# Local-global attention and a two-layer MLP on one core: q in 16-row partitions, a bank of its own for global-key scores, and a fixed order in two phases

## The chip, the cores and the metric

The kernel runs on one core of a Trainium2 chip. The metric is the device time of one execution in microseconds (us). TensorE runs the matmuls (PE in the profile, PEld its weight loads), VectorE is DVE, ScalarE is ACT, GpSimd is POOL, and SP issues the loads of v and the stores. TensorE's results go to PSUM, where the kernel's pools hold eight tiles of 128 x 512 fp32, called banks here.

## The reference

Eight batches of eight heads, 512 local and 32 global tokens of 64 features. Global queries look at all keys; local queries look at the 32 global keys and at local keys at most 32 positions away. The result goes through a two-layer MLP with weights 512 x 2048 and 2048 x 512.

```python
s_g  = scale * q_g @ [k_g, k_l].T;  out_g = softmax(s_g) @ [v_g, v_l]
s_ll = where(|i - j| <= 32, scale * q_l @ k_l.T, -1e9)
s_l  = concat([scale * q_l @ k_g.T, s_ll])
out_l = softmax(s_l) @ [v_g, v_l]
x = concat([out_g, out_l]) as [4352, 512]        # 8 * (32 + 512) rows
h = x @ w_in;  g = h / (1 + exp(-1.702 * h));  result = g @ w_out
```

## The kernel before

Four heads of a batch form a "quad", so there are 16 quads, two per batch. A quad does two rounds of score matmuls, three "value units" (`ov`: the sum of the exponentials, then the two halves of the features) and one output for the global queries (`og`). An "h step" makes 128 of the 2048 hidden features of 512 tokens (4 matmuls); an "o step" is a quarter of the sum for 128 output rows (4 matmuls). Batch i of x has 16 h steps and 16 o steps. The order of emission is reordered automatically per engine before it is built.

```python
psS = pool("psS", bufs=4, PSUM); psV = pool("psV", bufs=1, PSUM)      # scores; value units and og
psH = pool("psH", bufs=2, PSUM); psO = pool("psO", bufs=1, PSUM)      # h; o
qf = q_l.rearrange("b (u j) (n r t) d -> (b u) j r n (t d)", j=4, n=8, t=2)

def load(Q):
    for name, src in (("rk", kf), ("rq", qf)):
        r = ld.tile([128, 8, 2 * D], BF16, name=name)
        for j in range(4):
            nc.gpsimd.dma_start(out=r[32 * j : 32 * j + 32], in_=src[Q, j])

def load_v(Q):                       # ... loads vst from SP, then casts it:
    if Q < 4: nc.scalar.activation(v[:, :, : 4 * D], st, AF.Copy)
    else:     nc.gpsimd.tensor_copy(v[:, :, : 4 * D], st)

# start: load(0), globals, v0, load(1), masks, v1, w_in, load(2), v2, load(3), v3, w_out, ...

def quad(Q):                         # ... transposes of k and q, 2 rounds of scores
    for unit in range(3):
        ov = psV.tile([128, 512], F32, name="ov")
        for i, (e, q0, wd) in enumerate(pieces):       # global keys: 160, 160, 160, 32 columns
            nc.tensor.matmul(ov[:, q0 : q0 + wd], lhsT=lg, rhs=e, start=(i == 0), stop=False)
        for c in range(4):
            for j in range(4):                          # local keys, 32-column tiles
                nc.tensor.matmul(ov[32 * j : 32 * j + 32, q0 : q0 + wd], lhsT=lv, rhs=..., ...)
        # ... unit 0: reciprocal of the sums on VectorE; units 1, 2: product into x on VectorE

LAG = 24
for _ in batch(0): pass
for k in range(NBK * FC + LAG):
    i, st = divmod(k, FC)
    if i < NBK: h_step(i, st)
    if 0 <= k - LAG < NBK * FC: o_step(*divmod(k - LAG, FC))
    # ... and 12 pieces of the attention of batch i + 1, spread over the 16 steps;
    #     batch(b), from b = 1 on, expands the global keys of batch b + 1 with four products on GpSimd
```

The softmax here doesn't subtract the row's maximum and nothing guards it: scores larger than these inputs give would overflow.

## Time and profile before

| | before |
|---|---|
| time, median of the first 3 runs | 389.32 us (386.23 to 392.86) |
| TensorE busy | 347.3 us, 89% of the span |
| GpSimd busy | 135.8 us |
| period of one batch from 151 us on | 37.87 us |
| first h matmul / first o matmul starts | 36.95 / 77.8 us |

Lines of the page of before: busy time and instruction counts of each engine, then TensorE's busy tenths and its granted clock (in tenths) in 40 slices of about 9.7 us each, then the shares of the engines in the chain that ended last.

```profile
PE 347.3 (89%) x2960; PEld 178.4 (46%) x2960; DVE 223.8 (58%) x362; ACT 188.3 (48%) x375; POOL 135.8 (35%) x205
...
PE   0396777999999979999999999999999999999984
...
PEclk9999999899699998999999999999999999999999
...
PE 62%; DMA 11%; POOL 8%; ACT 8%; issue 6%; DVE 5%; ACTq 0%; DVEq 0%; POOLq 0%
```

Busy time of each engine of before in four stretches (from:to, length, then busy us and instruction count of each engine, the granted clock, the DMA share and GB/s).

```profile
core 0: us, PE busy (x) PEld busy (x) DVE busy (x) ACT busy (x) POOL busy (x), PEclk, DMA share, GB/s
0.00:30.00 30.00, 13.77 (x112) 8.15 (x116) 12.63 (x41) 13.19 (x21) 22.08 (x46) 1.00 1.25 181
30.00:75.00 45.00, 33.84 (x292) 17.32 (x285) 28.29 (x46) 17.06 (x35) 29.71 (x45) 0.96 1.16 132
75.00:151.00 76.00, 69.89 (x691) 36.11 (x689) 59.38 (x80) 40.73 (x84) 54.59 (x75) 0.93 0.80 104
151.00:209.00 58.00, 57.75 (x537) 29.65 (x538) 35.21 (x57) 32.32 (x67) 27.39 (x37) 1.00 0.54 93
```

From 151 us on TensorE has almost no idle time left (57.75 us busy of 58) and the clock is full. Before that it looks busy too, but this number misleads. The Trainium skill (Perfetto Trace Analysis, Identifying the Most-Contended Engine) says that matmul busy time is no good measure of distance from the limit, and here it isn't: between 75 and 151 us TensorE counts 69.89 us busy of 76, yet the matmuls that started in that stretch are worth only 58 us when each is counted at the pitch of the steady stage (0.864 us for four of 512 columns). The count of work is made from how many matmuls of each line have started by a moment:

| by, us | h, batches | o, batches | scores, quads | value units, quads |
|---|---|---|---|---|
| 30 | 0.00 | 0.00 | 2.00 | 0.17 |
| 50 | 0.19 | 0.00 | 2.00 | 2.00 |
| 75 | 1.00 | 0.00 | 3.59 | 2.33 |
| 151 | 2.59 | 1.06 | 8.00 | 7.00 |
| 209 | 4.12 | 2.62 | 10.84 | 10.00 |

A batch of h or of o is 13.8 us of streaming. The scores of a quad are about 1.84 us and its three value units about 2.2 us, read from the steady stage below (with the global output 0.56 us more, which I count with the units: 2.8).

The timeline of before in the steady stage, TensorE only (start, length, engine, line, operation, output<-inputs, shapes, count). A length runs to the modelled end of the last matmul, so the pitch is read from one start to the next.

```profile
216.23 0.23 PE L273 MATMUL ov<-e_2803,onesBD 128*128 128x160 bf16 x1
...
216.55 0.34 PE L280 MATMUL ov<-e_2803,ones_138 128*32 128x160 bf16 x8
...
216.97 1.04 PE L322 MATMUL hp<-xL,w_in_sb 128*128 128x512 bf16 x4
...
218.80 0.48 PE L231 MATMUL s<-qT,kT 32*128 32x192 bf16 x16
219.21 0.40 PE L253 MATMUL s<-qgBD_171,kT 128*128 128x128 bf16 x4
```

A value unit takes 216.97 - 216.23 = 0.74 us: 0.32 us for the four pieces with the global keys (`onesBD`), 0.42 us for the 16 tiled matmuls. Sixteen score matmuls take 219.21 - 218.80 = 0.41 us.

### The profile page before, as it was taken

The numbers are of one execution on the slowest core, as the hardware profiler recorded it, in microseconds if no ns is written. First come the engines' busy times: TensorE is split into PE (matmuls) and PEld (weight loads), VectorE is DVE, ScalarE is ACT, GpSimd is POOL, SyncE is SP. The second block draws the span as 40 slices with busy tenths as digits, with TensorE's granted clock in tenths as the row PEclk, the third lists the DMA queues.
The fourth block names the chain that finished last, engine by engine and source line by source line (L and its number), as shares of the span: only waits on it lengthen the run. The fifth ranks groups of instructions, "written<-read, shape, count | busy, mean of one in ns | idle before, by whom it ended". The sixth has DMA issues, their size and how long they took to land.

```text
span 389.2 us, 7403 instructions
## 1 busy us (share of the span) xinstructions
PE 347.3 (89%) x2960; PEld 178.4 (46%) x2960; DVE 223.8 (58%) x362; ACT 188.3 (48%) x375; POOL 135.8 (35%) x205
## 2 busy tenths in 40 slices
PE   0396777999999979999999999999999999999984
PEld 0253433544544434555555555555455544455531
DVE  4434359776797794658656855685545644333200
ACT  2462236625556843386448544854485443434311
POOL 8857937277890995826530011000000000000000
PEclk9999999899699998999999999999999999999999
DMA  9999999119992685936713000000101100111112
GB/s 155 190 189 179 112 185 145 12 34 175 172 106 59 104 116 57 135 83 83 112 51 83 29 28 29 29 29 28 49 7 38 45 29 27 40 43 54 53 57 54
DMA packets 83314, 31.15 MB, mean 80 GB/s; under 512 B 75856, under 2 KB 77904, under 8 KB 83280
## 3 DMA queue, kind: packets, MB, share of 16 engines
q0 software_dynamic: 44496, 13.38, 32.7%
q1 hardware_dynamic: 38784, 17.31, 18.3%
q8 instruction: 23, 0.38, 0.4%
q14 instruction: 11, 0.09, 0.1%
HBM read 35.13 MB, written 8.91 MB: 113 GB/s over the span
## 4 chain that ended last, share of the span: by engine, by line
PE 62%; DMA 11%; POOL 8%; ACT 8%; issue 6%; DVE 5%; ACTq 0%; DVEq 0%; POOLq 0%
PE op L337 26%; PE hp L322 21%; PE s L231 4%; DMA w_in_sb<-in_moe_w_in_dram 4%; PE ov L280 4%; PE s L253 4%; POOL rk L77 3%; POOL rq L77 3%; DMA rk<-in_k_l_dram 2%; DMA rq<-in_q_l_dram 2%; PE ov L273 2%; DMA w_out_sb<-in_moe_w_out_dram 2%; ACT ob L341 2%; ACT xg L305 2%; ACT th L325 2%
## 5 line engine op out<-in xcount | busy, mean ns | idle before, releaser
L322 PE MATMUL hp<-xL,w_in_sb 128*128 128x512 bf16 x512 | 136.9, 391 | 9.8 <-DVE gT L326 9.7
L337 PE MATMUL op<-w_out_sb,gT 128*128 128x512 bf16 x544 | 138.5, 381 | 3.7 <-ACT ob L341 2.8
L325 ACT ACTIVATE th<-hp 128x512 f32<-128x512 f32 (+1 forms) x144 | 83.0, 579 | 113.2 <-PE hp L322 111.2
L326 DVE SCALAR_TENSOR_TENSOR gT<-th,hp 128x512 bf16<-128x512 f32 (+1 forms) x144 | 93.4, 652 | 66.7 <-ACT th L325 66.1
L337 PEld LDWEIGHTS <-gT 128*128 128x128 bf16 x544 | 53.1, 98 | 67.5 <-issue 9.3
L322 PEld LDWEIGHTS <-w_in_sb 128*128 128x128 bf16 x576 | 53.3, 99 | 66.0 <-issue 16.9
L231 PE MATMUL s<-qT,kT 32*128 32x160 bf16 (+1 forms) x512 | 29.6, 252 | 16.8 <-DVE qT L216 14.2
L77 POOL DMA_DIRECT2D rk<-in_k_l_dram x64 | 37.2, 589 | 16.0 <-DVE kT L216 7.3
L77 POOL DMA_DIRECT2D rq<-in_q_l_dram x64 | 36.6, 577 | 8.2 <-DMA rq<-in_q_l_dram 3.0
L305 ACT ACTIVATE xg<-og,rg 32x64 bf16<-32x64 f32 x64 | 19.5, 305 | 30.2 <-DVE rg L301 29.6
L231 PEld LDWEIGHTS <-kT 32*128 32x128 bf16 x512 | 16.2, 96 | 33.5 <-issue 20.8
L341 ACT ACTIVATE ob<-op 128x512 f32<-128x512 f32 x34 | 20.5, 603 | 21.9 <-PE op L337 21.9
L293 DVE TENSOR_TENSOR xL<-ov,rs 128x512 bf16<-128x512 f32 x32 | 21.9, 686 | 8.3 <-PE ov L280 8.1
L216 DVE STREAM_TRANSPOSE kT<-rk 128x1024 bf16<-128x1024 bf16 x16 | 21.1, 1320 | 6.4 <-DMA rk<-in_k_l_dram 5.4
L216 DVE STREAM_TRANSPOSE qT<-rq 128x1024 bf16<-128x1024 bf16 x16 | 20.7, 1296 | 4.9 <-DMA rq<-in_q_l_dram 4.9
L287 DVE STREAM_TRANSPOSE sT<-ov 128x512 f32<-128x512 f32 x16 | 11.4, 711 | 7.6 <-PE ov L280 7.6
L306 DVE STREAM_TRANSPOSE xG<-xg 128x64 bf16<-128x64 bf16 x16 | 3.9, 246 | 19.8 <-ACT xg L305 19.8
L91 POOL CAST v_89<-vst 128x1024 bf16<-128x1024 f32 x3 | 3.1, 1040 | 28.3 <-issue 28.3
L291 DVE STREAM_TRANSPOSE rs<-rT 128x512 f32<-128x512 f32 x16 | 11.3, 708 | 0.5
L253 PEld LDWEIGHTS <-kT 128*128 128x128 bf16 x128 | 8.0, 100 | 7.6 <-issue 4.9
L186 POOL DMA_DIRECT2D w_in_sb<-in_moe_w_in_dram x16 | 8.5, 533 | 4.8 <-DMA w_in_sb<-in_moe_w_in_dram 4.3
L322 PE MATMUL hp<-xG,w_in_sb 128*128 128x256 bf16 x64 | 9.8, 273 | 0.1
(364 smaller groups left out, 347.9 us busy)
## 6 DMA issues: line engine op xcount, KB each, us to landing
vst<-in_v_l_dram SPq DMA_DIRECT2D x64, 128.0 KB, 4.6
out_dram<-ob SPq DMA_DIRECT2D x32, 256.0 KB, 2.0
rk<-in_k_l_dram POOLq DMA_DIRECT2D x64, 64.0 KB, 3.2
rq<-in_q_l_dram POOLq DMA_DIRECT2D x64, 64.0 KB, 3.7
w_in_sb<-in_moe_w_in_dram POOLq DMA_DIRECT2D x16, 128.0 KB, 7.1
w_out_sb<-in_moe_w_out_dram POOLq DMA_DIRECT2D x4, 512.0 KB, 9.2
out_dram<-ob SPq DMA_DIRECT2D x8, 64.0 KB, 1.7
rkg<-in_k_g_dram POOLq DMA_DIRECT2D x1, 192.0 KB, 12.6
```

The costliest lines, as they stand in the source:

```text
L77: nc.gpsimd.dma_start(out=r[32 * j : 32 * j + 32], in_=src[Q, j])
L216: nc.vector.transpose(dst.rearrange("p h (n r t) -> p h n t r", n=8, t=2), src.rearrange("p n (t h d) -> p h n t d", t=2, h=2),)
L231: nc.tensor.matmul(ps[j][:, col : col + wd], lhsT=kT[p, h, 128 * c : 128 * c + 128], rhs=qT[p, h, q0 : q0 + wd], start=(h == 0), stop=(h = ...
L253: nc.tensor.matmul(o, lhsT=l(h), rhs=r(h), start=(h == 0), stop=(h == 1), skip_group_check=True)
L280: nc.tensor.matmul(ov[32 * j : 32 * j + 32, q0 : q0 + wd], lhsT=lv, rhs=E[c // 2][:, j, col : col + wd], start=False, stop=(c == 3), skip_ ...
L293: nc.vector.tensor_mul(x[:, 2 * u + h, :], ov, rs)
L305: nc.scalar.activation(xg[p, :], og[p, j * D : (j + 1) * D], AF.Copy, scale=rg[p, j : j + 1])
L322: nc.tensor.matmul(hp[:, :n], lhsT=w_in_sb[:, kc, fc * 128 : (fc + 1) * 128], rhs=(xL[i] if i < B else xG)[:, kc, :], start=(kc == 0), sto ...
L325: nc.scalar.activation(th[:, :n], hp[:, :n], AF.Tanh, scale=0.851)
L326: nc.vector.scalar_tensor_tensor(gTs[i][:, fc, :n], in0=th[:, :n], scalar=1.0, in1=hp[:, :n], op0=ALU.add, op1=ALU.mult)
L337: nc.tensor.matmul(ops[i], lhsT=gTs[i][:, fc, tci * 128 : tci * 128 + 128], rhs=w_out_sb[:, fc, :], start=(fc == 0), stop=(fc == FC - 1))
L341: nc.scalar.activation(ob, ops[i], AF.Copy, scale=0.5)
```

## The change

Its intent: fewer and longer DMA runs for q, one 512-column matmul for global keys in place of pieces tucked into the score banks, GpSimd left to issue loads only, and a written-out order: all h steps of a batch, then its o steps mixed with the attention of the next batch. The diff, cut to its core:

```diff
+    ctx.enter_context(tc.manual_schedule())
-    psH = pool(bufs=2); psO = pool(bufs=1)
+    psM = pool(bufs=3)                       # h, o, and value units that ask for "M"
-    qf = q_l.rearrange("b (u j) (n r t) d -> (b u) j r n (t d)", j=4, n=8, t=2)
+    qf = q_l.rearrange("b (u j) (r t) d -> (b u) (j r) (t d)", j=4, t=16)
 ...
+        rq = ld.tile([128, 16 * D], BF16, name="rq")
+        nc.gpsimd.dma_start(out=rq, in_=qf[Q])              # one issue, 4 KB runs
 ...
+        nc.scalar.activation(v[:, :, : 4 * D], vst.pop(Q), AF.Copy)     # every V cast on ACT
+            nc.vector.tensor_mul(...)                                   # every expansion on VectorE
 ...  # loads at the start: w_in, w_out, and only then quads 2 and 3
-                            rhs=qT[p, h, q0 : q0 + wd],
+                            rhs=qT[p, h, :].rearrange("p (t r) -> p t r", t=16)[:, :, r0 : r0 + nr],
 ...
+        def K(self, kind="V"):               # scores with global keys: own bank
+            for h in range(2):
+                nc.tensor.matmul(self.kb, lhsT=self.G[0][:, self.u, h, :], rhs=self.q[:, h, :], ...)
 ...
+            nc.tensor.matmul(ov, lhsT=onesBD if unit == 0 else ..., rhs=self.ek, start=True, stop=False)
+            # 16 tiled matmuls into ov seen as [t, r]: runs of 10 or 12 columns
 ...  # output: four stores of 32 rows in place of one of 128
+    # prologue (batch 0): a.U(0, "M"), a.U(1, "M"), ... : value units in the three idle M banks
+    for i in range(B):
+        for fc in range(FC): h_step(i, fc)
+        if i + 1 < B: phase_o(i)             # o(i) mixed with the attention of batch i + 1
```

In `phase_o`, `o(k)` emits k o steps. For i = 0 and 1 the transposes, expansions and V casts of the next batch stand at the head of the phase ("late"); from i = 1 on those of the batch after it are spread over the phase ("ahead").

## The prediction

> What bounds it now. Two regimes. From 151 us to 343 us TensorE is busy 191.3 of 192 us at clock 1.00 (busy time by stretch), and the timeline repeats one batch every 37.87 us (same matmul at 205.08, 242.96, 280.82). Matmuls start at streaming pitch: 4 of 128x512 per 0.864 us. Per batch that is 64 h and 64 o matmuls, 27.6 us, plus two quads of attention at about 4.6 us each (two score rounds 1.84, three value units at 0.74, global output 0.56): 36.9 of 37.87. Nothing large can be won there by hiding work.
>
> From 0 to 151 us the kernel is starved. Only 170 of 576 h matmuls and 72 of 544 o matmuls have started by then; counted at the same pitches, with 3.65 batches of attention, that is 86 us of TensorE work in 151 us: 65 us lost. The chain of waits shows why: GpSimd issues (rk and rq, 0.58 us each, x128), DMA landings (rq, w_in, w_out, rk), casts and expansions queued in order on GpSimd; one GpSimd cast stands before an expansion at 125.7 us. The clock also falls to 0.50 at 100-105 us. The first scores wait until 13.5 us for q; batch 1 waits for q until 62.9 us; h runs 2.43 us per two steps there, because two h banks take turns (waits on gT).
>
> What the change does.
> 1. q load: one issue for four, 4 KB source runs for 512 B: saves about 48 GpSimd issues of 0.58 us (28 us of GpSimd) and most of 16,000 small packets. V casts (1.05 us) go to ACT and expansions (4 x 1.15 us per batch) to VectorE (0.5 us each), so GpSimd only issues. Weights come before batch 1; only two v loads compete with them.
> 2. Global-key scores in one bank: same columns; four value pieces become one. Pieces took 0.32 us against 0.216 for one 512-wide matmul: about 0.1 x 3 x 16 = 5 us saved, plus about 1 us in scores.
> 3. Fixed order: h phase 16 x 0.864 = 13.8 us. Three banks allow 2.59 us per bank against the 2.43 the chain needs, so it just stays TensorE-bound. Then o (13.8) with attention (8.5). Walking the order with trace durations, ACT about 18 and VectorE about 17 us fit in about 22.5 us, with about 1.3 us of bank and VectorE stalls: period 37.5, no real gain over 37.87.
> 4. Cost: output goes in 32-row stores, 4 times as many, off the path. q reads have runs of 10 to 12 elements, the value units write strided PSUM. The Trainium skill (SBUF — State Buffer, Door 1) says non-contiguous PSUM access slows matmuls significantly; no trace here shows it. I assume little, since runs are 40 to 48 bytes; doubling the units would cost 15 us.
>
> Sum (estimate from the durations above): first h at 28 us (37 before, and first batch then fully done), h(0) to 42, o with batch 1 in latency-bound order to 67, h(1) to 81, second such phase to 107; five periods of 37.6 to 295; h(7) 13.8, h(8) with o(7) 20.7, o(8) 7: 337; last store 4.6: 342. Plus about 4 us of low clock after sparse stretches: 346 us, an 11% gain, nearly all from before 151 us.
>
> Right if: h(2) starts near 107 us; GpSimd busy falls from 136 to under 90 us; period 37 to 38; no mean of value-unit matmuls above 0.30 us; software-queue packets fall by about 15,000.
>
> Wrong if: strided access slows matmuls (plus 10 to 25 us); fixed order leaves several us of stalls per phase; weights land later than 28 us and w_out later than 45 us; low clock persists.
>
> Predicted 346 us, range 334 to 364; faster 0.95, same 0.03, slower 0.02.

## More of the kernel before

The start of the value units of before, TensorE, with the idle time ahead of a row and what ended it in brackets.

```profile
29.74 0.48 PE L280 MATMUL ov<-e_296,ones_138 128*32 128x160 bf16 x8
...
31.34 0.29 PE L273 MATMUL ov<-e_296,vgU_156 128*128 128x160 bf16 x1 [0.83 <-DVE sT L287]
...
33.82 0.29 PE L273 MATMUL ov<-e_296,vgU_156 128*128 128x160 bf16 x1 [1.18 <-DVE xL L293]
...
35.91 0.59 PE L297 MATMUL og<-v_85,e_296 128*128 128x260 bf16 x2 [0.80 <-DVE xL L293]
...
36.95 1.06 PE L322 MATMUL hp<-xL,w_in_sb 128*128 128x512 bf16 x2
38.72 0.29 PE L273 MATMUL ov<-e_380,onesBD 128*128 128x160 bf16 x1 [0.71 <-ACT xg L305]
```

The local part of the first unit starts at 29.74 us; later units wait until VectorE, or once ScalarE, has finished with the only value bank (brackets), and the h matmuls of batch 0 begin only at 36.95 us, between units of quad 1.

## The result

The kernel after takes 355.50 us (353.54 to 356.88, 4 runs) against 389.62 us: ratio 0.9147, 95% interval 0.9065 to 0.9229. Here and below a ratio is the mean time of one kernel's runs over that of the other's runs of the same rounds, so it isn't quite the ratio of the medians that are quoted with it. Executions over 1.5% slower than the fastest of the same kernel are left out of the means. The ratio of 0.9147 comes out when the 392.86 us run of before is left out as slow; the median of 389.62 us still contains it. The time lies within the predicted range, 9.5 us above the predicted 346 us. All outputs are right.

The same lines of the page of after (slices of about 8.9 us here):

```profile
PE 321.5 (91%) x2720; PEld 154.0 (43%) x2720; DVE 227.7 (64%) x396; ACT 203.8 (57%) x403; POOL 70.8 (20%) x124
...
PE   0477997999769999999999999999999999999994
...
PEclk9999999999989999999999999999999999999999
...
PE 71%; DMA 12%; DVE 5%; POOL 5%; ACT 4%; issue 1%; POOLq 0%; DVEq 0%; ACTq 0%
```

GpSimd fell from 135.8 to 70.8 us busy and from 8% to 5% of the chain, and the tenths of PE reach 9 sooner. The same stretches of after, columns as for before:

```profile
0.00:30.00 30.00, 12.87 (x200) 7.22 (x201) 18.14 (x52) 12.65 (x25) 22.57 (x44) 1.00 0.97 150
30.00:75.00 45.00, 41.31 (x342) 19.23 (x341) 29.27 (x50) 26.21 (x54) 22.66 (x38) 1.00 1.27 186
75.00:151.00 76.00, 70.21 (x594) 32.70 (x593) 56.05 (x86) 47.42 (x91) 19.47 (x33) 0.98 0.61 94
151.00:209.00 58.00, 57.36 (x468) 26.76 (x466) 41.67 (x73) 36.74 (x72) 6.06 (x11) 1.00 0.48 89
```

The steady stage did not change: the first score matmuls of consecutive o phases start at 170.32 and 208.19 us, 37.87 us apart, exactly the period of before. So everything was won before it. The count of work shows where:

| by, us | h | o | scores | value units | after is ahead by, us of streaming (estimate) |
|---|---|---|---|---|---|
| 30 | 0.00 | 0.00 | 2.00 | 2.00 | 5 |
| 50 | 1.00 | 0.33 | 2.00 | 2.00 | 16 |
| 75 | 1.19 | 1.00 | 4.00 | 4.00 | 22 |
| 151 | 3.00 | 2.80 | 8.00 | 7.33 | 31 |
| 209 | 5.00 | 4.00 | 10.50 | 10.00 | 31 |

The last column multiplies the differences to the table of before by 13.8, 13.8, 1.84 and 2.8 us. Of the 34 us, 22 are won in the first 75 us and 9 more by 151 us. At 75 us both kernels have done about one batch of h; but after has done a whole batch of o, and before none.

The start of the value units of after:

```profile
21.46 0.63 PE L292 MATMUL ov<-ek,onesBD 128*128 128x512 bf16 x1
22.02 0.48 PE L298 MATMUL ov<-e_249,ones_129 128*32 128x160 bf16 x8
...
22.73 0.40 PE L292 MATMUL ov<-ek,vgU_147 128*128 128x512 bf16 x1
23.06 0.34 PE L298 MATMUL ov<-e_249,v_84 128*32 128x160 bf16 x8
...
27.72 0.34 PE L298 MATMUL ov<-e_400,ones_129 128*32 128x192 bf16 x8 [1.13 <-DVE e_400 L283]
...
30.03 0.59 PE L361 MATMUL hp<-xL,w_in_sb 128*128 128x512 bf16 x2
```

The local part of the first unit starts at 22.02 us, 7.7 us earlier, and no unit waits for a bank; the longest wait among the units, 1.13 us, is for the mask product on VectorE. h begins at 30.03 us.

One difference is not a wait. In before the unit at 38.72 us takes 0.52 us for its four pieces and then 0.71 us for its 16 tiled matmuls (the rows start at 38.72, 39.24 and 39.95 us). In the steady stage these take 0.32 and 0.42 us, and in after the global part takes 0.33 us already at 22.73 us. So TensorE streams at about 0.6 of its steady pace in the prologue of before, about 0.5 us more for each unit, although the clock column reads 1.00 there. What sets the pace was not tested, but it means that the clock column alone doesn't clear a stretch.

The steady stage of after, for comparison with the unit and the scores of before:

```profile
177.66 0.55 PE L245 MATMUL s<-qT,kT 32*128 32x160 bf16 x16
178.14 0.40 PE L260 MATMUL s<-qgBD_154,kT 128*128 128x128 bf16 x4
...
178.49 0.38 PE L292 MATMUL ov<-ek,onesBD 128*128 128x512 bf16 x1
178.80 0.34 PE L298 MATMUL ov<-e_2383,ones_129 128*32 128x160 bf16 x8
...
179.22 0.61 PE L374 MATMUL op<-w_out_sb,gT 128*128 128x512 bf16 x2
```

Sixteen score matmuls now take 178.14 - 177.66 = 0.48 us (0.41 before). The value unit takes 179.22 - 178.49 = 0.73 us (0.74 before): 0.31 us for the one wide matmul, 0.42 for the tiled ones.

### The profile page after: what moved, and what is told of

Its sections match the earlier page's. It is cut to its first block, busy times and chain, and to the rows that moved or that the text cites. A ratio compares the mean times of both kernels' runs of the same rounds, so it can differ in the third digit from the quotient of the medians.

```text
span 354.5 us, 6978 instructions
## 1 busy us (share of the span) xinstructions
PE 321.5 (91%) x2720; PEld 154.0 (43%) x2720; DVE 227.7 (64%) x396; ACT 203.8 (57%) x403; POOL 70.8 (20%) x124
## 3 DMA queue, kind: packets, MB, share of 16 engines
q0 software_dynamic: 29440, 13.38, 30.6%
## 4 chain that ended last, share of the span: by engine, by line
PE 71%; DMA 12%; DVE 5%; POOL 5%; ACT 4%; issue 1%; POOLq 0%; DVEq 0%; ACTq 0%
PE op L374 31%; PE hp L361 24%; DMA rq<-in_q_l_dram 6%; PE ov L298 5%; PE s L245 3%; DMA w_out_sb<-in_moe_w_out_dram 3%; PE ov L292 2%; PE s L260 2%; ACT xg L341 2%; DMA rk<-in_k_l_dram 2%; DMA w_in_sb<-in_moe_w_in_dram 2%; PE og L325 2%; DVE gT L366 2%; ACT th L365 2%; PE kb L274 1%; DVE kT L217 1%
## 5 line engine op out<-in xcount | busy, mean ns | idle before, releaser
L374 PE MATMUL op<-w_out_sb,gT 128*128 128x512 bf16 x544 | 133.1, 382 | 0.1
L361 PE MATMUL hp<-xL,w_in_sb 128*128 128x512 bf16 x512 | 113.4, 379 | 3.4 <-DVE gT L366 2.9
L365 ACT ACTIVATE th<-hp 128x512 f32<-128x512 f32 (+1 forms) x144 | 81.8, 574 | 42.6 <-PE hp L361 39.8
L361 PEld LDWEIGHTS <-w_in_sb 128*128 128x128 bf16 x576 | 56.2, 98 | 68.0 <-issue 6.2
L374 PEld LDWEIGHTS <-gT 128*128 128x128 bf16 x544 | 49.8, 98 | 54.0 <-issue 2.2
L245 PE MATMUL s<-qT,kT 32*128 32x160 bf16 (+1 forms) x512 | 19.7, 261 | 19.5 <-DVE qT L225 18.6
L245 PEld LDWEIGHTS <-kT 32*128 32x128 bf16 x512 | 10.6, 95 | 31.8 <-issue 13.3
L225 DVE STREAM_TRANSPOSE qT<-rq 128x1024 bf16<-128x1024 bf16 x16 | 19.3, 1204 | 0.9 <-DMA rq<-in_q_l_dram 0.8
L279 ACT ACTIVATE ek<-kb 128x512 bf16<-128x512 f32 x16 | 9.9, 616 | 12.3 <-PE kb L274 12.3
L77 POOL DMA_DIRECT2D rq<-in_q_l_dram x16 | 9.3, 583 | 7.8 <-DMA w_out_sb<-in_moe_w_out_dram 2.7
```

The lines of the kernel that those rows point to most:

```text
L225: nc.vector.transpose(qT.rearrange("p h (t r) -> p h t r", t=16), loaded[self.Q][1].rearrange("p (t h d) -> p h t d", t=16, h=2),)
L245: nc.tensor.matmul(ps[j][:, COL[c] : COL[c] + 16 * nr], lhsT=kT[p, h, 128 * c : 128 * c + 128], rhs=qT[p, h, :].rearrange("p (t r) -> p t ...
L361: nc.tensor.matmul(hp[:, :n], lhsT=w_in_sb[:, kc, fc * 128 : (fc + 1) * 128], rhs=(xL[i] if i < B else xG)[:, kc, :], start=(kc == 0), sto ...
L365: nc.scalar.activation(th[:, :n], hp[:, :n], AF.Tanh, scale=0.851)
L374: nc.tensor.matmul(ops[i], lhsT=gTs[i][:, fc, tci * 128 : tci * 128 + 128], rhs=w_out_sb[:, fc, :], start=(fc == 0), stop=(fc == FC - 1))
```

## The experiments

The theory with which they began (A) was the prediction's: the start starves because GpSimd has casts, expansions and loads in one in-order queue, behind which everything waits. Its rivals: the q layout itself (B); the automatic reordering itself (C). Later ones are named where they arise. Times are medians, ratios are to before in the same rounds; after stands at 0.9147. Some profiles of these runs lack a few per cent of the matmul records, so matmul counts come from complete profiles, and where a profile isn't complete (e5, e6, e7) from the weight loads, one for each matmul, whose records are complete.

| run | edit | time, us | ratio to before (95%) |
|---|---|---|---|
| e1_old_q | after, q as before | 356.98 | 0.9175 (0.9128 to 0.9222) |
| e2_pieces4 | after, wide value matmul in four | 356.04 | 0.9152 (0.9106 to 0.9198) |
| e3_before_manual | before, source order kept | 471.41 | 1.2115 (1.2061 to 1.2169) |
| e4_before_pool | before, GpSimd only issues | 391.83 | 1.0075 (1.0026 to 1.0123) |
| e5_before_lag16 | before, o right after h | 379.88 | 0.9771 (0.9726 to 0.9816) |
| e6_after_auto | after, automatic order | 372.58 | 0.9567 (0.9525 to 0.9608) |
| e7_after_wout | after, w_out loaded late | 364.28 | 0.9362 (0.9324 to 0.9399) |
| e8_early2 | after, transposes moved into h(0) | 359.88 | 0.9237 (0.9202 to 0.9273) |
| e9_before_all3 | before, three handicaps removed | 372.73 | 0.9561 (0.9517 to 0.9604) |
| e10_after_onev | after, prologue in one value bank | 364.15 | 0.9328 (0.9283 to 0.9372) |
| e11_early3 | after, batch 2's work spread | 351.94 | 0.9021 (0.8989 to 0.9053) |
| e12_early4 | after, heads of o phases reordered | 349.18 | 0.8945 (0.8919 to 0.8971) |

### e1_old_q: is it the q layout?

```diff
-    qf = q_l.rearrange("b (u j) (r t) d -> (b u) (j r) (t d)", j=4, t=16)
+    qf = q_l.rearrange("b (u j) (n r t) d -> (b u) j r n (t d)", j=4, n=8, t=2)
     # and with it four issues per load, the old transpose, contiguous score reads and
     # value writes, the old mask, one 128-row store
```

> The kernel after, with q loaded as before (four issues of 512 B runs per quad, token columns in natural order, contiguous score reads, contiguous value writes, 128-row stores). Theory A (the gain at the start comes from taking mixed work off GpSimd and from the new order of loads and stages, the q layout is a minor part): 354 to 362 us; software-queue packets back up by about 15,000 from 29,440; period of a batch 37.4 to 37.7 us instead of 37.87, because a round of 16 score matmuls takes 0.41 us instead of 0.48. Rival B (the q layout is what mended the start): 372 us or more, with h(1) starting 10 us later or more than at 74 us.

Measured 356.98 us, ratio 0.9175 against 0.9147 of after: a difference of 0.3%, within the intervals. Rival B falls. The layout did what it was meant to do (software-queue packets 44,544 with the old q, 29,440 in after), but this gave the kernel no time. Two small effects cancel: with the old q, h(1) begins about 1.4 us later (in the chain of waits its matmuls run without a stop from 77.00 us, in after from 75.63), and the period is 37.62 us (first scores at 170.17 and 207.79) instead of 37.87. The timeline of this run gives the cost of the strided score reads:

```profile
177.38 0.48 PE L245 MATMUL s<-qT,kT 32*128 32x160 bf16 x16
177.80 0.40 PE L260 MATMUL s<-qgBD,kT 128*128 128x128 bf16 x4
```

0.42 us for 16 matmuls with contiguous columns, 0.48 with runs of 10 or 12. Four rounds of scores per batch make that 0.25 us, which is the difference of the periods.

### e2_pieces4: what did one wide matmul save?

```diff
-            nc.tensor.matmul(ov, lhsT=..., rhs=self.ek, start=True, stop=False)
+            for i, (k0, kw) in enumerate(((0, 160), (160, 160), (320, 160), (480, 32))):
+                nc.tensor.matmul(ov[:, k0 : k0 + kw], lhsT=..., rhs=self.ek[:, k0 : k0 + kw],
+                                 start=(i == 0), stop=False)
```

> The kernel after, with the one 512-wide global-key matmul of each value unit cut in the four pieces of before (160, 160, 160, 32 columns). The prediction on record says that four pieces cost 0.1 us more per unit, 5 us in all: then 359 to 361 us and a unit of 0.83 us. Rival, from the trace of after where the unit still takes 0.73 us: the 0.1 us is the switch from the full array to the 32-column tiles, not the cutting: then within 0.8 us of after, unit 0.73 to 0.75 us.

356.04 us, ratio 0.9152: the pieces cost nothing. The 5 us of the prediction's second point don't exist. The wide matmul of after takes 0.31 us in its unit, not the 0.216 us that such a matmul takes among its like; the extra 0.1 us comes whether there is one matmul or four (0.32 us for the four in the steady stage of this run). That it belongs to the change from the full array to 32-column tiles is an inference. It agrees with the Trainium skill (TensorEngine Tiling (Array Packing), Key Properties), which says that a change of tiling mode drains the array, without giving a time.

### e3_before_manual: is a fixed order enough?

```diff
+    ctx.enter_context(tc.manual_schedule())        # in before, nothing else
```

> The kernel before with its source order kept as the order of emission and nothing else changed. Theory A (GpSimd's mixed queue and the load order starve the start): no better than before, 380 to 410 us, GpSimd still about 136 us busy. Rival C (the automatic reordering itself made the bad start, a fixed order is enough): 365 us or less.

471.41 us, 21% slower. Rival C, in the form "the reordering is to blame", falls. The order in which before's source stands is worse than the reordered one. VectorE in this run:

```profile
40.41 0.31 DVE L154 STREAM_TRANSPOSE kgT<-rkg 128x128 bf16<-128x128 bf16 x1 [26.08 <-DMA rkg<-in_k_g_dram]
...
42.21 1.29 DVE L217 STREAM_TRANSPOSE kT<-rk 128x1024 bf16<-128x1024 bf16 x1
```

The transposes of the globals of batch 1 stand ahead of those of quad 0 in the source; VectorE waits 26.08 us for their load, with quad 0's k (first issued at 1.4 us, landings of at most 6.2 us) long there, and quad 0's k and q are transposed only at 42.21 us.

### e4_before_pool: was GpSimd's mixed queue the cause?

```diff
-        if Q < 4:
-            nc.scalar.activation(v[:, :, : 4 * D], st, AF.Copy)
-        else:
-            nc.gpsimd.tensor_copy(v[:, :, : 4 * D], st)
+        nc.scalar.activation(v[:, :, : 4 * D], st, AF.Copy)
-            expand_g(b + 1, nc.gpsimd)
+            expand_g(b + 1, nc.vector)
```

> The kernel before with V casts on ACT and the expansions on VectorE, so that GpSimd only issues loads after the masks; order still automatic, q as before. Theory A: 360 to 375 us, since the waits behind GpSimd casts and expansions (for example 116 to 131 us in before) go. Rival C (the order of emission is what matters): within 2% of before, 382 to 397 us, with the stalls now behind other queues.

391.83 us, ratio 1.0075. GpSimd's busy time fell from 135.8 to 94.7 us and nothing was won. Theory A, on which the prediction's account of the start rests, falls in the form that clearing casts and expansions from GpSimd is enough. Where before's chain of waits has "issue" and expansions on GpSimd (116.7 to 131.2 us), the chain of this run has work of VectorE, ScalarE and TensorE instead. Two limits remain: the moved work stands in other queues, where the V casts on ScalarE waited 25.6 us for `og` between 36 and 155 us, and GpSimd still issues every load of k and q. This edit and the new q layout were not tried together in before.

The counts of work then gave theory D: TensorE lacks ready work at the start, and before withholds it. With `LAG = 24`, o(0) comes in the source only after half of h(1), and h(1) needs the attention of batch 1. So 13.8 us of o, ready once w_out has landed, cannot fill the wait for batch 1.

### e5_before_lag16: o as soon as it can be

```diff
-    LAG = 24
+    LAG = 16
```

> The kernel before with one number changed: the o steps follow the h steps of their batch at once (lag 16 steps) and no longer half a batch later (24). Theory D, formed after theory A fell: before is behind because in its first 150 us the o matmuls, which are ready filler, are held behind the second half of the next batch's h steps, and these wait for attention; at 75 us after has done a whole batch of o, before none, and both have done about the same of the rest. D expects 8 to 25 us less than before (364 to 381 us) with the first o matmul before 62 us. Rival E (the queue order of the loads and the automatic reordering keep PE short of any ready work): within 2% of before.

379.88 us, 9 us less for one number. Rival E is unlikely but not excluded, since the interval of the ratio (0.9726 to 0.9816) reaches across the 2% that it allows. The gain is at the low end of what D expected, and the first o matmul still starts at 77.1 us, not before 62. The gain comes later: by 151 us 1.67 batches of o are done against 1.06, scores and value units as in before. D is right that holding o back costs time, and wrong about when it does.

### e6_after_auto: is the fixed order needed?

```diff
-    ctx.enter_context(tc.manual_schedule())        # in after, nothing else
```

> The kernel after with the fixed order given up (automatic reordering as in before), source unchanged. Theory D (the gain lies in the stages and their order in the source, which the automatic order may largely keep): 350 to 368 us. Rival C (the automatic reordering is what cost the time): 375 us or more.

372.58 us: between the two expectations. The staged source alone, reordered automatically, is worth about 17 us over before; keeping its order is worth another 17 us. What the reordering did wrong shows on ACT:

```profile
36.43 1.06 ACT L90 ACTIVATE v<-vst 128x1024 bf16<-128x1024 f32 x1 [10.62 <-DMA vst<-in_v_l_dram]
37.39 1.25 ACT L340 ACTIVATE xg<-og,rg 32x64 bf16<-32x64 f32 x4
```

A V cast of a later quad was placed ahead of `xg` of quad 0. It waits 10.62 us for its load; `xg` waits behind it, and TensorE is idle for 10.15 us before its next matmul at 38.69 us. By 47 us after has finished h(0), this run a fifth of it.

### e7_after_wout: when does w_out have to be there?

```diff
+    load(2); load_g(2, 4); load(3)
     for g4 in range(4): ...                        # w_out
-    load(2); load_g(2, 4); load(3)
```

> The kernel after with the loads of quads 2 and 3 before those of w_out, as in before. If the early w_out is what lets o fill the wait for batch 1 (part of theory D): 3 to 8 us slower, o(0) starting near 55 us instead of 47. If DMA time is merely exchanged: within 1% of after.

364.28 us, 8 to 9 us slower (8.4 us by the ratios, 8.8 by the medians), just past the upper end. The first o matmul starts at 46.8 us, not near 55 as expected, but then o crawls: 0.20 of a batch by 55 us against 0.56 in after. So in after part of the gain is the place of w_out among the loads: the filler needs its weights.

### e10_after_onev: the banks of the prologue

```diff
-    a.U(0, "M"); a.U(1, "M"); ...                  # batch 0 only, both quads
+    a.U(0);      a.U(1);      ...                  # all in the one value bank
```

> The kernel after with the value units of the prologue (batch 0) all in the single value bank, as in before, instead of the three banks of the shared pool. Theory F (single bank makes each unit wait for the VectorE reader of the one before): first h matmul at 33 to 37 us instead of 30, and 3 to 7 us in all. Rival (prologue bound by ACT and VectorE, or by w_in): less than 1.5 us.

364.15 us, 7 us slower by the ratios, 8.7 by the medians. TensorE in the prologue of this run:

```profile
25.35 0.58 PE L292 MATMUL ov<-ek,vgU 128*128 128x512 bf16 x1 [0.82 <-DVE sT L307]
25.86 0.78 PE L298 MATMUL ov<-e,v 128*32 128x160 bf16 x16
26.57 0.78 PE L245 MATMUL s<-qT,kT 32*128 32x192 bf16 x16
...
38.93 1.03 PE L325 MATMUL og<-v,e 128*128 128x260 bf16 x4 [0.80 <-DVE xL L319]
...
39.96 4.31 PE L361 MATMUL hp<-xL,w_in_sb 128*128 128x512 bf16 x12
```

The first h matmul moved from 30.03 to 39.96 us. Units wait about 0.8 us for the reader of the one before (also at 34.75 and 36.84 us, not shown), and `og` does too, as in before; with one wait of 1.56 us for ScalarE these are 5.6 us. The pace is the slow one of before as well: 0.71 us for 16 tiled matmuls (25.86 to 26.57 us) where after takes 0.42. So the cost of one bank in this run is waits and slow pace together, which it doesn't separate. The Trainium skill (Perfetto Trace Analysis, Optimization Strategy) says that the same gap coming again and again can mean that there isn't enough SBUF or PSUM for the next tile, by the number of buffers for instance; these rows are a case of it. The three banks of the shared pool could not be in use for h or o meanwhile, since none was running.

### e9_before_all3: the three causes put into before

```diff
-            ov = psV.tile([128, 512], F32, name="ov")
+            ov = (psH.tile(..., tag="hp") if b == 0 else psV.tile(...))
-    LAG = 24
+    LAG = 16
     # and the loads of w_out moved ahead of those of quad 2
```

> The kernel before with three of its starting handicaps taken away and nothing else: o follows h at once (lag 16, as in the run before), the value units of batch 0 use the two h banks that are still idle instead of the single value bank, and w_out loads before quads 2 and 3. Theory F (the lost start has these three parts, about 9, 5 and 5 to 9 us, and they add up): 362 to 372 us. Rival G (with the automatic order the parts don't add, since it moves other work into the gaps or puts waits elsewhere): 375 us or more.

372.73 us, 17 to 18 us less than before and 7 to 8 us better than the lag alone: just outside the range of F and below that of G. The single effects would add to about 25 us if they were independent (9 from e5; 8 to 9 from e7; 7 to 9 from e10). So they are real but overlap or are partly lost again. The counts agree: at 75 us this kernel has done 0.62 batches of o where before had none, and at 90 us 0.97 against after's 1.19; but from there to 135 us it only goes from 0.97 to 1.44, after from 1.19 to 2.09. In its chain of waits between 109 and 133 us stand a GpSimd cast, a stretch named "issue", four GpSimd expansions, the loads behind them and the landing of q. This is the queue of theory A. Whether it is what remains between this kernel and after was not tried, and there is a rival: e6, which has everything of after but the fixed order, takes 372.58 us, the same as this kernel. The missing 17 us may as well be the order of emission.

### e8_early2 and e11_early3: moving work out of the heads of the o phases

TensorE in the second o phase of after, rows with idle time ahead of them:

```profile
90.76 0.55 PE L245 MATMUL s<-qT,kT 32*128 32x160 bf16 x16 [1.15 <-DVE qT L225]
91.79 0.38 PE L260 MATMUL s<-qgBD_162,kT 128*128 128x128 bf16 x4 [0.48 <-DVE qgBD_162 L165]
...
98.83 0.55 PE L245 MATMUL s<-qT,kT 32*128 32x160 bf16 x16 [1.54 <-DVE qT L225]
...
101.89 0.49 PE L298 MATMUL ov<-e_1350,ones_129 128*32 128x192 bf16 x8 [1.59 <-DVE e_1350 L283]
```

Transposes and expansions of batch 2 stand at the head of this phase, although its loads had landed long before: after issues the last load of quad 5 at 58.66 us. The phase takes from 86.85 us (first o matmul) to 118.07 us (first h matmul of batch 2), 31.2 us; the steady one takes 193.80 - 170.32 = 23.5 us. Two kernels moved the work.

```diff
     # e8: quads 2 and 3 load before w_out; after step 11 of h(0):
+            if i == 0 and fc == 11:
+                nq[1][0].Tk(), nq[1][0].Tq(); transpose_g(2, 4); expand_g(1)
+                nq[1][1].Tk(), nq[1][1].Tq()
     # and the same for batch 2 in one block at the end of the first o phase
```

> The kernel after with the work on k, q and the global keys of batches 1 and 2 (VectorE transposes and expansions, V casts) taken out of the head of the o phases: batch 1's is done in the middle of h(0) (quads 2 and 3 load before w_out), batch 2's at the end of the first o phase, so that both first o phases start as the later ones do. In after, the stretches 47 to 61 us and 88 to 106 us hold the stalls of these heads, about 4 and 6 us. Expected: 345 to 350 us if they lie on the critical path; if w_out lands later than the end of h(0) the first gain is lost: 349 to 352 us.

359.88 us: worse than after, and worse than expected. VectorE and TensorE in h(0) of this run:

```profile
42.38 1.31 DVE L217 STREAM_TRANSPOSE kT<-rk 128x1024 bf16<-128x1024 bf16 x1
...
47.61 1.19 DVE L225 STREAM_TRANSPOSE qT<-rq 128x1024 bf16<-128x1024 bf16 x1
...
49.42 1.87 PE L361 MATMUL hp<-xL,w_in_sb 128*128 128x512 bf16 x4 [5.72 <-DVE gT L366]
49.42 0.10 PEld L361 LDWEIGHTS <-w_in_sb 128*128 128x128 bf16 x1 [6.01 <-issue]
```

In an h phase VectorE has 0.18 us to spare of each 0.864 us step, so 6 us of transposes and expansions in one block stop h itself: TensorE idles 5.72 us. This kernel also has the late w_out of e7. Against e7, with the same order of loads, it is 4 to 5 us faster (359.88 against 364.28 us; 0.9237 against 0.9362), so moving the work paid even so, and less than the late w_out cost.

```diff
     # e11: batch 2's transposes, expansions and casts one by one between
     # the VectorE work of the first o phase; loads in the order of after
+        if first: a2.Tk()      # after the mask of the second quad's second round
+        ...                    # a2.Tq(), c2.Tk(), expansions, c2.Tq() further on
```

> The kernel after with batch 2's transposes, expansions and V casts spread over the first o phase (VectorE idles about 10 us there) instead of at the head of the second, whose head holds about 5 us of TensorE idle time. Expected: 350 to 353 us if the first phase has room; 354 to 358 us if the moved VectorE work delays h(1), as it did when it stood in one block.

351.94 us, as expected: ratio 0.9021, 1.4% better than after by the ratios.

### e12_early4: only the order within the head

```diff
+        if late and not first: c.Tk(), c.Tq()       # into VectorE's 3 us of waiting
         a.S(0)
+        X4(a)                                       # exponentials ahead of the o group
         o(1)
         a.K()
-        X4(a)
         a.XK()
         a.M(0)
-        if late: c.Tk(), c.Tq()
+        if first: c.Tk(), c.Tq()
```

> The kernel after with two moves of emission at the head of the o phases: the exponentials of the first score round go ahead of the o group and its copy on ACT, and in the second o phase the second quad's transposes go before the first scores, into the 3 us that VectorE idles there. The stalls of 1.54 and 1.59 us at 98.8 and 101.9 us should go: 351 to 354 us, 0.5 to 1% less than after. If they only move on: same as after within 0.4%.

349.18 us (348.72 to 349.47), ratio 0.8945: 1.8% better than after by the medians, 2.2% by the ratios, and more than expected. What TensorE waited for from 83 to 114 us, in order of size (total us, times, longest):

```profile
PE s L245 <- DVE qT L225: 1.2, 1, 1.2
...
PE ov L298 <- DVE e L283: 0.2, 1, 0.2
```

The two stalls of 1.54 and 1.59 us are gone or down to 0.24 us. h(2) starts at 111.14 us instead of 118.07: 2.4 us are won by the time the second phase sends its first scores (88.40 instead of 90.76 us), the other 4.5 us within it. That is more than the two stalls. In after the clock column stands at 0.50 from 101.5 to 104.5 us, around the end of the second one, and the 8 o matmuls from 102.31 us take 2.91 us; in this run the clock stays at 1.00 and the same eight take 1.73 us (from 96.56 us). The period after that is 37.87 us as ever (first scores at 163.39 and 201.26 us). This is the fastest kernel.

## Why the prediction was right, and where it was wrong

Right in the time and in the place, and partly by luck: the cause that it names for the start did not hold, while its timetable has the order of work that did the good. 355.5 us is within 334 to 364. The prediction said that the gain would come nearly all from before 151 us and that the steady period would not move (37 to 38 us; 37.87 measured). Packets fell by 15,056 (predicted about 15,000) and GpSimd's busy time to 70.8 us (predicted under 90).

- **"What the change does", point 1, the cause of the start: wrong.** It read the chain of waits (issues, casts and expansions on GpSimd) as the cause. Moving casts and expansions alone won nothing (e4, ratio 1.0075), and undoing the q layout in after cost 0.3% (e1). In their place the runs show: value units of batch 0 in three banks rather than one (e10, 7 to 9 us), w_out loaded early enough to let o fill the wait (e7, 8 to 9 us), o(i) not held behind h(i+1) (e5, 9 us), and an emission order that keeps load-dependent work from standing ahead of ready work (e6, 17 us in all; one such stall of 10.15 us is seen in its trace). These overlap and must not be added. The prediction has the early weights, o beside the attention of batch 1 and the fixed order in its timetable, but puts no price on any of them, and it doesn't name the three value banks.
- **Point 2, 5 us for fewer value pieces and about 1 us in the scores: wrong.** Measured 0.00 to 0.01 us per unit (0.74 to 0.73) and no loss with four pieces (e2). It compared four pieces ahead of tiled matmuls with a wide matmul among wide ones. The scores did not get cheaper either: in the steady stage those of a quad take 1.97 us (0.83 and 0.71 for the two rounds, 0.43 for the bank of global keys) against 1.88 before (0.95 and 0.93).
- **Point 3, the timetable: right in kind, too short.** First h at 30.0 us (predicted 28), h(1) at 72.6 (67), h(2) at 118.1 (107), then five periods of 37.87 (37.6) to 307.4 us, and 47 us more as predicted (295 to 342). So the o phases at the start were mis-sized: 9 of the 11 us at h(2) arise between the first h and h(2). The second phase takes 31.2 us where 26 were allowed, because the head of that phase makes TensorE wait for VectorE and ACT in order (e12 takes most of this away); the prediction names such stalls among its "wrong if". The 4 us that were added for low clock did not come on top, which hid part of the miss.
- **Point 4, strided access: right that it matters little.** Strided PSUM writes in the value units cost nothing (0.42 us for 16 in both kernels), strided reads of q 0.06 to 0.07 us per 16 matmuls. The check that no value-unit mean exceeds 0.30 us was badly worded: most of the tiled ones are at 0.23 to 0.25 (up to 0.37 where the pace is slow), but any 512-wide matmul is listed at about 0.38.

Left open: how much of the remaining 17 us between e9 and after is GpSimd's queue and how much the fixed order; how much of the prologue's gain is the faster pace of the matmuls; and how much of the poor stretch from 75 to 151 us in before is the clock (0.93 on average there, 0.98 in after), which no run isolates.

## What to carry to other kernels

When an engine looks busy but the kernel is slow, count the work started by a few moments in each kernel; a chain of waits names one chain of several, and removing its links one by one may win nothing. At a start, look for ready work that is held back by order (filler behind work that isn't ready), by its own operands (weights loaded last) or by a bank although others lie idle. A fixed order pays only if its source puts nothing that waits for a load, or for a slow reader, ahead of work that is ready: the same switch made one source 21% slower and the other 4% faster.

## What the Trainium skill lacked or had wrong

- SBUF — State Buffer, Door 1 says that any non-contiguous PSUM access slows matmuls significantly. Here 16 tiled value matmuls that write runs of 10 or 12 fp32 columns, each run a whole number of the 8-byte lines that the page names, take 0.42 us, the same as with contiguous columns in before.
- The same page gives no cost in time for a matmul's moving operand read in short runs. Here runs of 10 or 12 bf16 elements take 0.48 us for 16 score matmuls, contiguous ones 0.41 to 0.42 us (before, e1).
- TensorEngine Tiling (Array Packing), Key Properties says that a change of tiling mode drains the array, with no time. Here a 512-wide full-array matmul ahead of tiled ones takes 0.31 us against 0.216 us among its like; e2 shows that the 0.1 us isn't the number of pieces.
- TensorE: Matmul & The Clock Gate, Back-to-back issue gap gives about 131 ns per matmul as the sustained rate at 512 columns with weight loads. Here the steady stage shows 216 ns (0.864 us for four) at a granted clock of 1.00, the figure that the page calls the isolated gap.
- The same page, What's actually happening, has the clock fall to half after an idle window of about 3.4 us. In before it is 0.50 from 99.5 to 105 us, although TensorE's longest idle time between 88 and 100 us was 0.93 us; the matmuls of the 10.2 us from 88.6 us on are worth about 7 us at the steady pitch (estimate). In after it is 0.50 from 101.5 to 104.5 us, around the end of an idle time of 1.59 us. Neither has one idle time of that length before it.
